# A second load of x and the cut of the last output-weight loads, in a one-core attention and expert decode kernel

Two small things were changed in a long kernel: the residual's x is taken from rows that are already on chip instead of being loaded a second time, and the last two blocks of the output weight are loaded in halves.

## Chip, cores and metric

One core of one Trainium2 chip. The metric is device time in microseconds (us), the median of several executions. Most executions of a kernel agree within 0.3%; the verdict "faster" or "slower" needs 2%.

## The reference, cut to what matters

Four tokens (B = 4), D = 1024, 32 heads of 128, a cache of 8192 positions per head, an expert with F = 3584. One token attends to the whole cache, so K and V are read once each: 537 MB of the 576 MB that the kernel reads.

```python
q = x @ wq                                    # (4, 32, 128)
p = softmax(q . k_cache * 128 ** -0.5)        # over 8192 positions
a = (p . v_cache) @ wo
y = (silu(x @ w_gate) * (x @ w_up)) @ w_down * sigmoid(x @ w_r)
b = x + y                                     # the residual
g = sigmoid((x * gate_w).sum(-1))
return g * a + (1 - g) * b
```

The change touches the term `(1 - g) * x` and the end of the product with `wo`.

## The kernel before

All large loads go through one ring of five 4 MB slots (`slot()`), and all of them are issued by SyncE's sequencer (`nc.sync.dma_start`), one after the other in the order of the built program. A K piece or a V piece covers two heads and fills one slot. VectorE transposes a K piece in four steps into buffers `T` of the pool `ttp`, which has two buffers under one tag; TensorE multiplies each transposed part into `S_ps`. After every eighth K piece a softmax follows.

```python
ring = ctx.enter_context(tc.tile_pool(name="ring", bufs=5))
ttp = ctx.enter_context(tc.tile_pool(name="ttp", bufs=2))
...
x6 = ttp.tile([NX, D], BF, name="x6", tag="T")
nc.scalar.dma_start(out=x6[0:Bn], in_=x2)              # x, used at the start
...
def k_piece(u):
    ...
    kn = slot()
    nc.sync.dma_start(out=kn[:], in_=kv_view(A_k_cache, u))
    for c in range(JR // CJ):                          # four steps
        T = ttp.tile([P, CJ, 2, 32, 2], BF, name="T", tag="T")
        nc.vector.transpose(out=T[:]..., in_=kn[:, c * CJ * Dh:(c + 1) * CJ * Dh]...)
        ...                                            # 8 matmuls into S_ps
    if t == GT - 1:
        softmax(g)
```

The residual is added once, in mid-kernel, after K piece 32, the first of a group of heads. It loads x again, into a buffer of the same two-deep pool:

```python
def add_x():
    xs = ttp.tile([Bn, 3 * D], BF, name="xs", tag="T")
    xb, xf = xs[:, 0:D], xs[:, D:3 * D].bitcast(F32)
    nc.sync.dma_start(out=xb, in_=x2)
    nc.vector.tensor_copy(out=xf, in_=xb)
    for n in range(NH):
        mm_acc(acc[:, n * NB:(n + 1) * NB], dg[:], xf[:, n * NB:(n + 1) * NB])
...
    if (kind, u) == ("k", NT // 2):
        add_x()
```

At the end, eight blocks of `wo` (1 MB each, four rows `r` per partition) are multiplied by the attention output. Each row takes two matmuls. The last block comes as three rows and one row:

```python
last = [wo_block(g) for g in range(2, NWB - 1)]
last += [wo_block(NWB - 1, 0, FR - 1), wo_block(NWB - 1, FR - 1, FR)]
...
for use in last:
    use()
```

## Time and profile before

| | before |
|---|---|
| median | 1360.24 us (1360.13 to 1360.25, three executions; a fourth, in the table of the result below, took 1360.83) |
| profiled execution | 1359.36 us, span 1357.7 us |
| read from HBM | 575.69 MB, 424 GB/s over the span |
| busy: TensorE, VectorE | 78%, 47% |

Two parts of the profile page of the kernel before. The first lines are the span and the busy time of the engines; the two rows below cut the span into 40 equal slices (33.9 us each), DMA being the busy share of the 16 DMA engines in tenths, GB/s what they moved.

```profile
span 1357.7 us, 8253 instructions
...
PE 1061.2 (78%) x4600; PEld 231.9 (17%) x2412; DVE 631.8 (47%) x375; ACT 41.5 (3%) x46; POOL 48.1 (4%) x115
...
DMA  9999999999999999997999999999999999999998
GB/s 406 427 431 430 431 431 432 431 430 432 430 430 432 431 432 431 433 430 342 385 432 433 431 427 431 431 429 430 432 432 432 432 431 431 432 430 430 431 426 338
```

The stream of loads is the bound: 430 to 433 GB/s in nearly every slice. Slices 19 and 20 (342 and 385) are a hole in the middle, slice 40 is the end.

The waits of the sequencer that issues the loads, in the kernel before: issue line, what it waited for, total us, times, longest.

```profile
engine line waited for: us in total, times, longest us
SPq L396 <- DVE T L338: 540.2, 55, 20.4
SPq L335 <- PE o_ps L403: 424.1, 50, 9.1
...
SPq L208 <- DVE T L338: 42.4, 1, 42.4
...
SPq L208 <- PE S_ps L344: 2.3, 1, 2.3
```

The first two rows look large and are harmless: a sequencer that waits for a ring slot while four other loads are under way loses nothing. The reload of x (L208) waited once, for 42.4 us and then 2.3 us more, with fewer loads under way than usual, as the timeline of the same sequencer shows (start, duration, what was issued). What it waited for is its buffer: the trace has the end of the third transpose of K32 at 644.88 us, and of the matmuls that read it at 647.24 us.

```profile
590.62 0.33 SPq L335 DMA_DIRECT2D piece<-in_A_k_cache_dram  x1
602.19 0.33 SPq L396 DMA_DIRECT2D piece<-in_A_v_cache_dram  x1
647.27 0.32 SPq L208 DMA_DIRECT2D xs<-in_A_x_dram  x1
647.64 0.35 SPq L335 DMA_DIRECT2D piece<-in_A_k_cache_dram  x1
648.05 0.42 SPq L396 DMA_DIRECT2D piece<-in_A_v_cache_dram  x1
648.51 0.43 SPq L335 DMA_DIRECT2D piece<-in_A_k_cache_dram  x1
649.04 0.46 SPq L396 DMA_DIRECT2D piece<-in_A_v_cache_dram  x1
```

K32 was issued at 590.62 and V24 at 602.19. Then the reload stood at the head of the order until 647.27. The four loads behind it left within 2 us of it, so their slots had been free for some time.

What that did to the stream, in stretches (length, busy time of each engine, granted clock, DMA share, GB/s), kernel before:

```profile
core 0: us, PE busy (x) PEld busy (x) DVE busy (x) ACT busy (x) POOL busy (x), PEclk, DMA share, GB/s
400.00:634.00 234.00, 190.68 (x792) 42.03 (x407) 115.83 (x67) 6.56 (x9) 6.36 (x17) 0.92 1.00 431
634.00:655.00 21.00, 15.37 (x60) 4.34 (x37) 10.03 (x7) 1.73 (x1) 2.52 (x3) 0.78 0.51 204
655.00:700.00 45.00, 35.34 (x145) 7.02 (x72) 18.02 (x8) 0.00 (x0) 0.53 (x2) 0.92 1.00 431
```

And the end, TensorE's matmuls with the last blocks of `wo` (start, duration, matmuls, in brackets the idle time before and what ended it):

```profile
1350.92 3.75 PE L188 MATMUL acc<-piece,LT 128*4 128x512 bf16 x16 [0.59 <-DMA piece<-in_A_wo_dram]
```

Block 6 and both parts of block 7 run as one row of 16 matmuls.

### The profile page before, as it was taken

The numbers are of one execution on the slowest core, as the hardware profiler recorded it, in microseconds if no ns is written. First come the engines' busy times: TensorE is split into PE (matmuls) and PEld (weight loads), VectorE is DVE, ScalarE is ACT, GpSimd is POOL, SyncE is SP. The second block draws the span as 40 slices with busy tenths as digits, with TensorE's granted clock in tenths as the row PEclk, the third lists the DMA queues.
The fourth block names the chain that finished last, engine by engine and source line by source line (L and its number), as shares of the span: only waits on it lengthen the run. The fifth ranks groups of instructions, "written<-read, shape, count | busy, mean of one in ns | idle before, by whom it ended". The sixth has DMA issues, their size and how long they took to land.

```text
span 1357.7 us, 8253 instructions
## 1 busy us (share of the span) xinstructions
PE 1061.2 (78%) x4600; PEld 231.9 (17%) x2412; DVE 631.8 (47%) x375; ACT 41.5 (3%) x46; POOL 48.1 (4%) x115
## 2 busy tenths in 40 slices
PE   3667779876988879886877769788787859887778
PEld 1111111211111111211111111111111112111111
DVE  3555654545544455445354455445454445456000
ACT  0000010001000000001000010000100010000000
POOL 2000000000000000000000000000000000000000
PEclk9878889887989979898988989898799988989999
DMA  9999999999999999997999999999999999999998
GB/s 406 427 431 430 431 431 432 431 430 432 430 430 432 431 432 431 433 430 342 385 432 433 431 427 431 431 429 430 432 432 432 432 431 431 432 430 430 431 426 338
DMA packets 22025, 576.23 MB, mean 424 GB/s; under 512 B 2386, under 2 KB 2394, under 8 KB 2660
## 3 DMA queue, kind: packets, MB, share of 16 engines
q1 hardware_dynamic: 21968, 575.69, 98.8%
q8 instruction: 27, 0.44, 0.1%
q14 instruction: 10, 0.08, 0.0%
q10 hardware_dynamic: 20, 0.02, 0.0%
HBM read 575.69 MB, written 0.01 MB: 424 GB/s over the span
## 4 chain that ended last, share of the span: by engine, by line
DMA 49%; PE 31%; DVE 12%; issue 6%; POOL 1%; ACT 1%; SPq 0%; DVEq 0%; ACTq 0%
DMA piece<-in_A_k_cache_dram 42%; PE o_ps L403 15%; PE S_ps L344 14%; DVE T L338 10%; DMA piece<-in_A_v_cache_dram 5%; DMA piece<-in_A_wo_dram 1%; PE small L421 1%; POOL PB L375 1%; DVE PT L369 1%; ACT PTs L367 1%; ACT OS L413 1%; DVE OS L414 1%; PE acc L188 0%; POOL tot L379 0%; DVE m L355 0%
## 5 line engine op out<-in xcount | busy, mean ns | idle before, releaser
L338 DVE STREAM_TRANSPOSE T<-piece 128x2048 uint32<-128x2048 uint32 x256 | 576.2, 2289 | 444.8 <-DMA piece<-in_A_k_cache_dram 292.6
L344 PE MATMUL S_ps<-T,Z 128*128 128x512 bf16 x2048 | 549.6, 419 | 252.4 <-DVE T L338 241.9
L403 PE MATMUL o_ps<-piece,PB 128*16 128x512 bf16 x2048 | 455.0, 380 | 17.2 <-DMA piece<-in_A_v_cache_dram 17.2
L344 PEld LDWEIGHTS <-Z 128*128 128x128 bf16 x1024 | 108.5, 106 | 677.7 <-issue 674.7
L403 PEld LDWEIGHTS <-PB 128*16 128x16 bf16 x1024 | 91.6, 90 | 373.7 <-issue 361.9
L414 DVE SCALAR_TENSOR_TENSOR OS<-o_ps,mE,OS 128x512 f32<-128x512 f32 x16 | 12.0, 751 | 175.8 <-ACT OS L413 175.8
L328 POOL TENSOR_TENSOR Z<-qa,mq 128x16 bf16<-128x16 bf16 x64 | 16.8, 264 | 1084.7 <-PE S_ps L344 1067.0
L413 ACT ACTIVATE OS<-o_ps,mE 128x512 f32<-128x512 f32 x16 | 11.0, 687 | 1049.0 <-PE o_ps L403 1049.0
L421 PEld LDWEIGHTS small<-selg,OS 128*128 128x128 f32 x128 | 22.9, 253 | 12.0 <-issue 11.1
L421 PE MATMUL small<-selg,OS 128*128 128x8 f32 x128 | 20.6, 288 | 0.0
L355 DVE TENSOR_REDUCE m<-S_ps 128x1 f32<-128x1024 f32 x8 | 9.8, 1225 | 15.9 <-PE S_ps L344 15.9
L188 PE MATMUL acc<-piece,LT 128*4 128x512 bf16 x64 | 14.9, 378 | 1.9 <-DMA piece<-in_A_wo_dram 1.8
L375 POOL COPY PB<-PT 64x1024 bf16<-64x1024 bf16 x8 | 15.1, 1889 | 28.8 <-DVE rex L377 28.8
L374 ACT COPY PB<-PT 64x1024 bf16<-64x1024 bf16 x8 | 15.3, 1909 | 10.6 <-DVE PT L369 10.6
L369 DVE STREAM_TRANSPOSE PT<-PTs 128x1024 bf16<-128x1024 bf16 x8 | 10.0, 1245 | 12.0 <-ACT PTs L367 12.0
L188 PE MATMUL acc<-piece,hT 128*4 128x512 bf16 x56 | 12.4, 379 | 0.0
L131 PE MATMUL small<-identb,x 6*128 6x6 bf16 x8 | 0.6, 192 | 14.1 <-DVE identb L128 14.1
L381 DVE RECIPROCAL rinv<-tot 128x16 f32<-128x16 f32 x8 | 2.0, 253 | 19.9 <-POOL tot L379 19.9
L367 ACT ACTIVATE PTs<-S_ps,negm 128x1024 bf16<-128x1024 f32 x8 | 8.9, 1114 | 70.8 <-DVE negm L364 70.8
L227 PE MATMUL S_ps<-piece,xw 128*4 128x512 bf16 x64 | 7.2, 626 | 2.7 <-DMA piece<-in_A_wq_dram 2.7
L424 DVE SCALAR_TENSOR_TENSOR OT<-small,sgb,rinv 128x8 bf16<-128x8 f32 x16 | 3.2, 202 | 10.2 <-PE small L421 10.2
L360 POOL PARTITION_ALL_REDUCE gmx<-mex x8 | 3.1, 392 | 79.7 <-issue 42.1
(72 smaller groups left out, 75.7 us busy)
## 6 DMA issues: line engine op xcount, KB each, us to landing
piece<-in_A_k_cache_dram SPq DMA_DIRECT2D x64, 4096.0 KB, 39.1
piece<-in_A_v_cache_dram SPq DMA_DIRECT2D x63, 4096.0 KB, 38.4
piece<-in_A_wq_dram SPq DMA_DIRECT2D x2, 4096.0 KB, 22.1
piece<-in_B_w_gate_dram SPq DMA_DIRECT2D x2, 3584.0 KB, 39.7
piece<-in_B_w_up_dram SPq DMA_DIRECT2D x2, 3584.0 KB, 33.9
piece<-in_A_wo_dram SPq DMA_DIRECT2D x7, 1024.0 KB, 27.3
piece<-in_B_w_down_dram SPq DMA_DIRECT2D x1, 4096.0 KB, 36.3
piece<-in_A_v_cache_dram SPq DMA_DIRECT2D x4, 1024.0 KB, 32.6
```

Of the source, the lines that this page charges most:

```text
L188: nc.tensor.matmul(out_ap, lhsT=lhsT, rhs=rhs, start=start, stop=True, skip_group_check=True)
L328: nc.gpsimd.tensor_tensor(out=Z[:, :, 31:31 + P].rearrange("p e (s d c) -> p e s d c", s=HT, d=QH)[:, :, :, :, 0], in0=qa[:, :, h0:h0 + HT ...
L338: nc.vector.transpose(out=T[:].rearrange("p j h i e -> p (j h i e)").bitcast(U32), in_=kn[:, c * CJ * Dh:(c + 1) * CJ * Dh].bitcast(U32))
L344: nc.tensor.matmul(sps[:, z, :], lhsT=Z[:, he, s:s + P], rhs=T[:, 16 * z:16 * z + 16, half, :, e], start=(t == 0 and c == 0 and he == 0), ...
L367: nc.scalar.activation(out=PTs[:], in_=sps[:].rearrange("p z n -> p (z n)"), func=ACT.Exp, bias=negm[:, 0:1], scale=scale, accum_out=rs[:, ...
L369: nc.vector.transpose(out=PT[:].rearrange("p j i -> p (j i)"), in_=PTs[:])
L374: nc.scalar.copy(out=Bv[0:W, :, :, 0, :], in_=Pv[0:W])
L375: nc.gpsimd.tensor_copy(out=Bv[W:P, :, :, 1, :], in_=Pv[W:P])
L403: nc.tensor.matmul(o_ps[row:row + NM, e, :], lhsT=B_[:, JT * t + c, z, w].rearrange("p e s j -> p (e s j)"), rhs=vn[:, j0 * Dh:(j0 + 4) * ...
L413: nc.scalar.activation(out=o_sb[:], in_=o_ps[:, 0, :], func=ACT.Copy, scale=mE[:, 0:1])
L414: nc.vector.scalar_tensor_tensor(out=o_sb[:], in0=o_ps[:, 1, :], scalar=mE[:, 1:2], in1=o_sb[:], op0=ALU.mult, op1=ALU.add)
L421: nc.tensor.matmul(oT[:, :], lhsT=o_sb[:, q * Dh:(q + 1) * Dh], rhs=selg[:, q].rearrange("p t s -> p (t s)"), start=(q == 0), stop=(q == 3))
```

## The change

The intent: no second load of x, so that nothing but ring loads stands in the load order; and less work after the last landing.

```diff
-    x6 = ttp.tile([NX, D], BF, name="x6", tag="T")
+    x6 = const.tile([NX, D], BF)
...
     def add_x():
-        xs = ttp.tile([Bn, 3 * D], BF, name="xs", tag="T")
-        xb, xf = xs[:, 0:D], xs[:, D:3 * D].bitcast(F32)
-        nc.sync.dma_start(out=xb, in_=x2)
-        nc.vector.tensor_copy(out=xf, in_=xb)
+        xf = ttp.tile([Bn, D], F32, name="xf", tag="T")
+        nc.vector.tensor_copy(out=xf[:], in_=x6[0:Bn])
...
-    last = [wo_block(g) for g in range(2, NWB - 1)]
-    last += [wo_block(NWB - 1, 0, FR - 1), wo_block(NWB - 1, FR - 1, FR)]
+    last = [wo_block(g) for g in range(2, NWB - 2)]
+    last += [wo_block(g, r, r + FR // 2) for g in (NWB - 2, NWB - 1) for r in (0, FR // 2)]
```

Only the one load is gone and one more `wo` load is there.

## The prediction

> **What bounds the kernel.** The load stream. The slices of the profile page show the 16 DMA engines at 90% or more nearly everywhere, moving 430 to 433 GB/s (576 MB in all), while TensorE is busy 78% of the span and VectorE 47%. The Trainium skill, "DMA: Bandwidth & Descriptors", section "Specifications", gives a fabric ceiling of 435 GB/s; the trace agrees to 1%. Time is won only where the stream pauses: at the start (406 GB/s in slice 1), at the end (338 in slice 40), and in one hole in the middle (342 and 385 in slices 19 and 20).
>
> **The hole.** All K, V and weight loads are issued in order from one sequencer. The residual's reload of x (8 KB) stands in that order, and its destination is a buffer of the two-deep ring that the K transposes use. The waits of the DMA-issuing sequencer show that this one issue waited 42.4 + 2.3 us for VectorE and TensorE to get through the following K piece. The timeline of that sequencer: a V load at 602.19 us, then nothing until the x load at 647.27; four 4 MB loads follow within 1.8 us, so several ring slots had been free already. The stream ran dry at 640.6 us. The stretch 634 to 655 us moved 204 GB/s instead of 431: (431 - 204)/431 x 21 us = 11.1 us lost. From 655 to 700 us it is 431 again, so nothing is made up later. The same page, section "Anatomy of one DMA", says that semaphore waits happen on the issuing sequencer before dispatch; the trace agrees.
>
> **What the change does there.** It removes the load, its issue (0.32 us) and, above all, its wait at the head of the in-order issues. The cast (0.68 us) and four small matmuls (1.9 us) remain at the same places in VectorE's and TensorE's order, and lie under the stream. Other group boundaries, with the same softmax but no x load, keep 430 to 432 GB/s, so I expect no pause in place of the hole. Gain: 11.1 us, all on the critical path.
>
> **The tail.** Before, blocks 6 and 7 of wo come as 1 MB, 768 KB and 256 KB. Block 6 lands at 1350.88 us; its 8 matmuls and the 8 of block 7 run back to back from 1350.92 to 1354.67 (0.215 us apart); the last landings are at 1352.74 and 1353.38. With halves, TensorE has done four matmuls earlier, and the last four wait for the last landing instead: 1353.4 + 4 x 0.215 + 0.2 = 1354.5. Gain 0.2 us; between -0.5 and +0.6. The additional issue costs nothing: loads are issued 15 us ahead.
>
> **Sum.** 1360.24 - 11.1 - 0.2 = 1348.9 us, 0.8% less. Range 1346.5 to 1352.0. Faster by over 2%: 1%; within 2%: 98%; slower by over 2%: 1%.
>
> **What would show it right.** Slices 19 and 20 at 430 or more; K and V issues near 611 and 629 us where none was; mean rate 427 GB/s; in the tail, the last four matmuls follow a DMA wait.
>
> **What would make it wrong.** A pause that remains at this softmax boundary, with cast and matmuls in it, would leave several us. Another chip whose steady rate differs by 0.3% moves the time by 4 us. In the tail, 4 KB rows might stream worse than 6 or 8 KB ones, below 1 us.

## The result, and the profile after

| | before | after |
|---|---|---|
| median | 1360.24 us (1360.13 to 1360.83) | 1349.57 us (1349.41 to 1349.65) |
| profiled execution | 1359.36 us, span 1357.7 us | 1349.57 us, span 1347.8 us |
| HBM rate over the span | 424 GB/s | 427 GB/s |

The medians differ by 10.67 us. The ratio is 0.9921 (95% interval 0.9903 to 0.9938); such ratios are the mean time of one kernel's fast runs over that of the other's in the same rounds, so not quite the ratio of the medians. The interval excludes 1.

The rows of slices of the page, after:

```profile
DMA  9999999999999999999999999999999999999997
GB/s 403 433 433 422 433 430 430 432 433 430 430 433 430 430 431 434 429 431 432 433 428 432 433 430 430 433 431 429 432 434 429 428 433 434 429 428 434 432 423 323
```

Slices 19 and 20 are now 431 and 432. The waits of the load sequencer, after:

```profile
SPq L394 <- DVE T L336: 551.3, 57, 21.0
SPq L333 <- PE o_ps L401: 442.1, 52, 10.4
```

The long wait of L208 is gone, and the two waits for ring slots have grown by 11 and 18 us in total. Its timeline, after:

```profile
590.53 0.33 SPq L333 DMA_DIRECT2D piece<-in_A_k_cache_dram  x1
603.21 0.33 SPq L394 DMA_DIRECT2D piece<-in_A_v_cache_dram  x1
612.17 0.33 SPq L333 DMA_DIRECT2D piece<-in_A_k_cache_dram  x1
620.43 0.33 SPq L394 DMA_DIRECT2D piece<-in_A_v_cache_dram  x1
629.39 0.33 SPq L333 DMA_DIRECT2D piece<-in_A_k_cache_dram  x1
649.78 0.33 SPq L394 DMA_DIRECT2D piece<-in_A_v_cache_dram  x1
```

K33, V25 and K34 are now issued at 612, 620 and 629 us, where nothing was. The following gap of 20 us before V26 does no harm, because three pieces (K33, V25 and K34) are still under way when it ends. The stretch of the hole, after:

```profile
634.00:655.00 21.00, 15.74 (x52) 4.48 (x33) 13.17 (x9) 1.67 (x1) 2.45 (x3) 0.67 1.00 430
```

And the end, after:

```profile
1338.79 3.61 PE L188 MATMUL acc<-piece,LT 128*4 128x512 bf16 x16 [0.58 <-DMA piece<-in_A_wo_dram]
1342.57 1.02 PE L188 MATMUL acc<-piece,LT 128*4 128x512 bf16 x4 [0.17 <-DMA piece<-in_A_wo_dram]
1343.81 1.02 PE L188 MATMUL acc<-piece,LT 128*4 128x512 bf16 x4 [0.22 <-DMA piece<-in_A_wo_dram]
```

The two halves of block 7 are now waited for, 0.17 and 0.22 us each.

**Where 9.8 us went, execution against execution.** In the traces each large load raises its semaphore (the counter that those who need the data wait for) in 16 steps, which I take for one from each of the 16 DMA engines; the packed trace has the time of each step. From these come the first and the last landing of a load. No view of the profile prints them; the table is worked out from the traces of the two profiled executions.

| | before | after |
|---|---|---|
| V24, last of 16 engines landed | 640.6 us | 640.5 us |
| K33, last landed | 659.9 | 650.2 |
| last load of all, last landed | 1353.38 | 1343.77 |
| from there to the end of the span | 4.27 | 4.07 |

In a steady stream a piece lands 9.7 us after the one before. Before, K33 landed 19.36 us after V24, so the hole cost 9.65 us; at the last load the two kernels are 9.61 us apart. With 0.2 us at the end this makes 9.8 us; the two profiled executions differ by 9.79 us. The medians differ by 0.88 us more because the profiled execution of the kernel before was that much faster than its median.

### The profile page after: what moved, and what is told of

It reads as the page before. It is cut to its first block, busy times and chain, and to the rows that moved or that the text cites. A ratio compares the mean times of both kernels' runs of the same rounds, so it can differ in the third digit from the quotient of the medians.

```text
span 1347.8 us, 8253 instructions
## 1 busy us (share of the span) xinstructions
PE 1059.3 (79%) x4600; PEld 233.2 (17%) x2412; DVE 631.4 (47%) x375; ACT 41.5 (3%) x46; POOL 47.9 (4%) x115
## 4 chain that ended last, share of the span: by engine, by line
DMA 50%; PE 30%; DVE 11%; issue 6%; ACT 1%; POOL 1%; SPq 0%; DVEq 0%; ACTq 0%
DMA piece<-in_A_k_cache_dram 40%; PE o_ps L401 16%; PE S_ps L342 13%; DVE T L336 10%; DMA piece<-in_A_v_cache_dram 9%; PE small L419 1%; DMA piece<-in_A_wo_dram 1%; POOL PB L373 1%; DVE PT L367 1%; ACT PTs L365 1%; ACT OS L411 1%; DVE OS L412 1%; POOL tot L377 0%; PE acc L188 0%; PE o_ps L225 0%
## 5 line engine op out<-in xcount | busy, mean ns | idle before, releaser
L342 PEld LDWEIGHTS <-Z 128*128 128x128 bf16 x1024 | 108.0, 105 | 667.2 <-issue 664.3
L419 PEld LDWEIGHTS small<-selg,OS 128*128 128x128 f32 x128 | 24.9, 273 | 12.2 <-issue 11.1
L422 DVE SCALAR_TENSOR_TENSOR OT<-small,sgb,rinv 128x8 bf16<-128x8 f32 x16 | 3.2, 202 | 11.7 <-PE small L419 11.7
```

What stands on the lines that cost most here:

```text
L342: nc.tensor.matmul(sps[:, z, :], lhsT=Z[:, he, s:s + P], rhs=T[:, 16 * z:16 * z + 16, half, :, e], start=(t == 0 and c == 0 and he == 0), ...
L419: nc.tensor.matmul(oT[:, :], lhsT=o_sb[:, q * Dh:(q + 1) * Dh], rhs=selg[:, q].rearrange("p t s -> p (t s)"), start=(q == 0), stop=(q == 3))
```

## The experiments

Twelve runs were made, of nine different kernels, in three sets of four, each set on one chip beside the kernel before. All results were correct. In the order of the sets, the kernel before had medians of 1361.16 us (1358.78 to 1362.74), 1362.23 (1360.15 to 1364.05) and 1361.54 (1360.14 to 1362.73).

| run | kernel | median us | range |
|---|---|---|---|
| e1_control | the change | 1349.59 | 1349.34 to 1349.70 |
| e2_x_only | first part alone | 1349.49 | 1349.36 to 1349.80 |
| e3_tail_only | second part alone | 1360.19 | 1358.85 to 1360.69 |
| e4_tail_211 | the change, last block 2+1+1 rows | 1349.26 | 1349.18 to 1349.78 |
| e5_own_buffer | reload without a wait | 1349.47 | 1349.37 to 1349.78 |
| e6_act_queue | reload issued by ScalarE | 1349.48 | 1349.41 to 1349.50 |
| e7_mid_group | reload four K pieces later | 1355.23 | 1354.22 to 1356.36 |
| e8_before_again | before, one execution | 1363.81 | one run, state unknown |
| t1_whole | the change, last two blocks whole | 1350.03 | 1349.98 to 1350.27 |
| t2_three_one | the kernel of e2 again | 1349.55 | 1349.48 to 1349.65 |
| t3_halves | the change again | 1349.61 | 1349.46 to 1349.92 |
| t4_two_one_one | the kernel of e4 again | 1349.19 | 1348.95 to 1349.29 |

**The theory:** the reload waited for a buffer at the head of an in-order line of loads, and the stream behind it ran dry. **Rivals:** the reload itself (traffic, latency) disturbs the stream; VectorE and TensorE waiting for x make the hole; the pool's rotation, with x of the start in it, makes it; the gain comes from the tail.

### Which part of the change

e1 is the change as it stands. e2 has only the diff's parts for x, e3 only the last four lines of the diff.

> The changed kernel once more, as the control of this set. Theory (in-order issue): ratio to before 0.992, that is 10.5 to 11 us less, with both parts of the change in it. Rival (the chip or run differed): a ratio nearer to 1.

> Only the first part: x from the rows on chip, wo blocks 6 and 7 as before (1 MB, 768 KB, 256 KB). Theory: the whole gain is here, within 0.3 us of the control: 1349.6 us, 10.3 to 11.1 us below before; the 634 to 655 us stretch at 430 GB/s. The prediction's tail term says this is 0.2 us slower than the control; the profile of the changed kernel, in which the last 1 MB of the stream arrived 1.1 us late against the rest, allows the contrary: up to 0.9 us faster than the control.

> Only the second part: the reload of x stays, wo blocks 6 and 7 come in halves. Theory: 1360.0 us, -0.2 us from before (between -0.6 and +0.6), and the hole of 11 us near 640 us stays. If the gain came from the tail, 1349.6 us.

Measured: ratios to before of 0.9915, 0.9915 (0.9901 to 0.9928) and 0.9991 (0.9979 to 1.0004). The whole gain is in x. Set against the median of before on the same chip, e1 and e2 gained 11.6 and 11.7 us, more than the 10.5 to 11 and the 10.3 to 11.1 us that I had expected, since before scatters (below). e3 keeps the hole (208 GB/s from 634 to 655 us in its trace, and a wait of 42.4 + 2.1 us at the reload). The second part is worth nothing that these runs can tell.

### Load, wait or place

e5 starts from the change and puts the reload back on the same sequencer, into a buffer that nothing else uses:

```diff
+        xb = const.tile([Bn, D], BF, name="xb")
         xf = ttp.tile([Bn, D], F32, name="xf", tag="T")
-        nc.vector.tensor_copy(out=xf[:], in_=x6[0:Bn])
+        nc.sync.dma_start(out=xb[:], in_=x2)
+        nc.vector.tensor_copy(out=xf[:], in_=xb[:])
```

> The second load of x is back, on the same sequencer and at the same place in its order, but into a buffer of its own, so that it waits for no engine. Theory (the wait at the head of the in-order issues made the hole): no hole, 1349.6 us, within 0.3 us of the changed kernel. Rival (the load itself, its 8 KB in small packets and its latency, disturbs the stream): 1360 us.

Measured: 1349.47 us; the reload was issued at 591.0 us, and the stretch 634 to 655 us ran at 429 GB/s:

```profile
634.00:655.00 21.00, 15.58 (x62) 4.34 (x38) 14.26 (x9) 1.53 (x1) 2.31 (x3) 0.79 1.00 429
```

The load itself costs nothing, although it landed only at 630.3 us, 39.3 us after its issue and within a microsecond of the K piece issued just before it. One thing more differs from the kernel before: here the built program has the reload ahead of V24, as the source has it; before, it stood behind V24. A reload without a wait at exactly the old place was not run; e6 leaves the order of the large loads as it was.

e6 starts from the kernel before (with `wo` in halves) and changes one word:

```diff
-        nc.sync.dma_start(out=xb, in_=x2)
+        nc.scalar.dma_start(out=xb, in_=x2)
```

> The second load of x is as before, into the two-deep ring and with x of the start in that ring too, but ScalarE's sequencer issues it. Its wait is then the same, some 40 us, but nothing of the stream stands behind it. Theory: no hole, 1349.6 us, within 0.5 us of the changed kernel, although VectorE still waits 1 to 3 us for the landing. Rivals (VectorE's and TensorE's wait for x, or the ring's rotation with x in it, made the hole): 1360 us.

Measured: 1349.48 us, 428 GB/s from 634 to 655 us:

```profile
634.00:655.00 21.00, 12.28 (x40) 3.77 (x24) 9.60 (x8) 1.91 (x1) 2.59 (x3) 0.67 1.00 428
```

The instructions on the tile of x in this run (line, engine, duration in ns min/median/max, first and last start; below, VectorE's idle time that ended with the landing):

```profile
L208 ACTq DMA_DIRECT2D xs<-in_A_x_dram x1: 254/254/254, 649.7 to 649.7; - x1
L209 DVE CAST xs<-xs x1: 682/682/682, 655.9 to 655.9; 4x1024 f32<-4x1024 bf16 x1
...
  DMA xs<-in_A_x_dram: 5.7, 1
```

Issued at 649.7, x was not cast until 655.9: the landing took about 6 us beside the running stream, VectorE waited 5.7 us for it and TensorE's weight load 5.2 us for VectorE. In the kernel before these two waits were 1.1 and 0.6 us, and I had expected 1 to 3 us here; the longer ones cost nothing in the total. So the compute engines' wait and the pool's rotation are not the cause: here x of the start is in the pool as before. Only the place of the wait, in front of the stream's loads, is left.

e7 also starts from the kernel before with halves, and moves the addition:

```diff
-        if (kind, u) == ("k", NT // 2):
+        if (kind, u) == ("k", NT // 2 + 4):
```

> The second load of x is as before (ring, same sequencer), but the addition of x stands four K pieces later, in the middle of a group of heads, where no softmax holds VectorE up between the landing of the K piece and its transposes. wo in halves. Theory: the sequencer still waits until the K piece is nearly computed, some 9.5 us after it landed, when the next V piece has just landed (9.7 us later), so a short hole stays: about 2.2 us in the last landings, 1351.8 us (1350.5 to 1354). Rival (any second load costs the same 10 us wherever it stands): 1360 us. The spread between the first and the last of the 16 engines to land a load should fall to about 0.5 us after this hole, and be 3 to 3.5 us at the end.

Measured: 1355.23 us. The rival "10 us wherever it stands" is wrong, but so was my number; the runs, from 1354.22 us on, touch neither 1351.8 nor the range up to 1354 that I gave. The load sequencer and the stretches around the reload:

```profile
681.68 0.33 SPq L396 DMA_DIRECT2D piece<-in_A_v_cache_dram  x1
721.78 0.33 SPq L208 DMA_DIRECT2D xs<-in_A_x_dram  x1
722.16 0.34 SPq L335 DMA_DIRECT2D piece<-in_A_k_cache_dram  x1
```

```profile
700.00:710.00 10.00, 7.36 (x34) 1.53 (x17) 1.83 (x2) 0.69 (x1) 0.26 (x1) 0.99 0.99 426
710.00:724.00 14.00, 12.27 (x40) 3.71 (x23) 8.69 (x6) 0.00 (x0) 0.00 (x0) 0.64 0.55 216
```

V28 landed last at 718.5 us, and the reload left at 721.78, 12.9 us after VectorE had begun to transpose K36 (708.92); I had expected 9.5 us from the landing. TensorE's granted clock was 0.64 in that stretch, where I had counted on full clock. The next piece landed at 734.35, 6.1 us later than a steady stream would have brought it. The sign and the order of the mechanism hold; the size depends on a compute speed that I took from a favourable stretch.

### Why the kernel before scatters and the changed one does not

> The kernel before once more, for a second trace of it: in the set with the control its runs lay between 1358.8 and 1362.7 us, while those of the changed kernel lay within 0.4 us. Theory: the hole's length varies with the compute it waits for, so its last-landing loss is 9.7 us plus whatever this run is above 1359.4 us, within 0.4 us; the stream elsewhere is the same within 0.3 us.

Measured: 1363.81 us, 4.45 us above the profiled execution of before. Its reload left at 651.90 us, 4.63 us later than before's 647.27. V24 landed last at 640.5 and K33 at 664.3: with the steady 9.7 us taken off, the hole cost 14.1 us, against 9.7 + 4.45 = 14.15 expected. Without their holes the two spans are the same, 1348.0 us, so the stream elsewhere did not differ, as expected. TensorE around the K piece that the reload waits for, in the profiled execution of before and then in e8:

```profile
638.96 3.57 PE L344 MATMUL S_ps<-T,Z 128*128 128x512 bf16 x8 [9.55 <-DVE T L338]
642.33 1.43 PE L421 MATMUL small<-selg,OS 128*128 128x8 f32 x8
643.61 3.63 PE L344 MATMUL S_ps<-T,Z 128*128 128x512 bf16 x16
```

```profile
641.20 3.57 PE L344 MATMUL S_ps<-T,Z 128*128 128x512 bf16 x8 [9.54 <-DVE T L338]
644.57 1.71 PE L421 MATMUL small<-selg,OS 128*128 128x8 f32 x8
646.13 5.73 PE L344 MATMUL S_ps<-T,Z 128*128 128x512 bf16 x16
```

The piece started 2.2 us later in e8, and stayed at half clock longer. The clock records of the trace (the share of the full TensorE clock that was granted, with the time of each change) give a stretch at 0.5 from 633.08 to 643.32 us in the first and from 636.79 to 650.44 us in the second. The late start goes back to the clock too: in e8 a stretch at 0.5 from 612.90 to 619.72 us lies on the matmuls of K31, which ended 2.2 us later than in before, where the clock was full (means of 0.69 and 1.00 from 611 to 622 us). The Trainium skill, "TensorE: Matmul & The Clock Gate", section "Part 1: The HAM clock gate", says that an idle window of about 3.4 us brings the half rate, that a busy one ends it, and that the window runs free of the kernel. These traces agree: the stretches at 0.5 are 10.24 and 13.65 us long, three and four times 3.41, after TensorE had been idle for some 9.5 us during the softmax. One busy window did not always end it: in e8 the clock rose 9.2 us after the first matmul, though TensorE was busy without a break from 642 to 650 us; in before it rose 4.4 us after it. In the kernel before, the length of the hole is set by this compute, so in these two traces the clock accounts for the 4.6 us between the two reloads, and so for the difference of the totals. The trace of e3, which has the hole too, fits: 10.24 us at half clock, the reload at 647.03, 1358.85 us in all. That the whole scatter of before, from 1358.78 to 1364.05 us in the three sets, comes from there is likely but not shown: its other executions were not traced, and no run held the clock. The changed kernel and e2, e5 and e6, in which nothing in the load order waits that way, all lie between 1349.3 and 1349.9. e8 is a single execution; its sums are taken inside one trace.

### The skew of the 16 engines

From the same landings: time between the first and the last of the 16 engines to land one load.

| us between first and last landing | near 630 to 640 us | next load | near 1290 us |
|---|---|---|---|
| before (hole at 640) | 3.4 | 0.5 | 3.5 |
| after | 3.4 | 3.4 | 6.6 |
| e7 (hole at 718) | 3.4 | 3.7 | 3.3 |

A hole brings the engines together; I read it so that the fast ones run out of work first and wait. In e7 the spread fell from 3.6 to 0.6 us at its hole, and grew to 3.3 again, as expected. The growth is not steady. In before the spread stands at 2.0 us from 700 to 1089 us and at 3.5 us from 1110 us on; between, one load adds 1.6 us, and after the hole one load (landed at 700.26) adds 1.5 us. Each of these two steps meets a packet of 16 KB on another queue, at 1098.1 and 694.6 us. The page counts such packets as instruction loads (queue and kind, packets, MB, share of the engines):

```profile
q8 instruction: 27, 0.44, 0.1%
q14 instruction: 10, 0.08, 0.0%
```

In the traces of before, after and all twelve runs, each of the 109 steps of more than 0.15 us (from 60 us on) has one of these packets, of 8 or 16 KB, between the first landing of the load before and the last landing of its own. Of all 1998 loads in these traces only 667, a third, have one there. So instruction loads go with the drift; that they cause it is not shown, as no run changed them. The spread is why the mean rate overstates the hole: in the stretch 634 to 655 us the bytes missing are worth 11.1 us, but part of it is fast engines stopping up to 3.4 us early, and those were ahead anyway. What counts is the last engine, 9.6 us. By bytes, the changed kernel is 10.9 us ahead at 574 MB and only 9.6 us ahead at the last landing of a load; the 1.3 us is the larger spread at its end (6.5 against 3.5 us).

### The tail, all cuts on one chip

The edits to the changed kernel, for t1 and t4 (e4):

```diff
-    last = [wo_block(g) for g in range(2, NWB - 2)]
-    last += [wo_block(g, r, r + FR // 2) for g in (NWB - 2, NWB - 1) for r in (0, FR // 2)]
+    last = [wo_block(g) for g in range(2, NWB)]                            # t1
+    last = [wo_block(g) for g in range(2, NWB - 2)]                        # t4
+    cuts = [(NWB - 2, 0, 2), (NWB - 2, 2, 4), (NWB - 1, 0, 2), (NWB - 1, 2, 3), (NWB - 1, 3, 4)]
+    last += [wo_block(*cut) for cut in cuts]
```

> The changed kernel with the last wo block cut in 2, 1 and 1 rows instead of 2 and 2: after the last landing two matmuls remain instead of four (0.215 us each), so 0.4 us less than the control if the last landing is what the end waits for and does not move: 1349.2 us. If more and smaller loads at the end land later, no gain or a loss of some tenths.

> The changed kernel with wo blocks 6 and 7 each loaded whole (1 MB). Theory of the tail: eight matmuls, 0.215 us apart, follow the last landing instead of four, so 0.86 us more than the changed kernel: 1350.4 us. If the end is not bound by the last landing plus its matmuls: 1349.5 us.

> x from the rows on chip, last block 3 rows and 1 row as in the kernel before (the same kernel as the run with the first part alone), again beside the others. Theory: the eight matmuls of block 7 run behind those of block 6 and end 1.28 us after the last landing began to be usable, against 1.07 us with halves: 0.2 us more than the changed kernel; the earlier set showed no difference (1349.49 against 1349.59 us).

> The changed kernel again, as the control of this set: 1349.5 us.

> Last block in 2, 1 and 1 rows, again beside the others. Theory: two matmuls after the last landing instead of four, 0.3 to 0.4 us less than the control of this set; the earlier set showed 0.33 us.

| last block | last landing us | to the start of the last matmul | to the end of the span | median us |
|---|---|---|---|---|
| whole (t1) | 1343.54 | 1.55 | 4.74 | 1350.03 |
| 3 + 1 (t2) | 1343.71 | 0.91 | 4.21 | 1349.55 |
| halves (t3) | 1343.81 | 0.69 | 4.06 | 1349.61 |
| 2 + 1 + 1 (t4) | 1343.90 | 0.26 | 3.68 | 1349.19 |

The number of matmuls after the last landing does what was expected: halves against whole is 0.86 us up to the last matmul, of which 0.68 us is left at the end of the span. But each finer cut of these four had its last landing 0.1 to 0.2 us later in its trace. The other traces of the same kernels do not settle whether that is chance: 1343.76 for 3 + 1 (e2), 1343.57 and 1343.77 for halves (e1 and the changed kernel), 1343.90 for 2 + 1 + 1 (e4). In the medians, whole costs 0.42 us, not 0.86; 3 + 1 and halves cannot be told apart (0.06 and, in the first set, 0.10 us in favour of 3 + 1, inside ranges of 0.2 to 0.5 us). The cut 2 + 1 + 1 is 0.42 us below halves, with ranges that do not meet; in the first set it was 0.33 us, with one of its four runs above the control's. It is the version that beats both kernels, the changed one by a few tenths.

## Why the prediction was right, point by point

- **The bound and the cause: right.** The time went where the stream paused; the cuts at the end are worth tenths. e5 and e6 take away the wait at the head of the loads and nothing else of weight, and each gives the whole gain. The prediction rests here on the Trainium skill, "DMA: Bandwidth & Descriptors", "Anatomy of one DMA" (a wait for a semaphore happens on the issuing sequencer). That section is written for DMAs issued by GpSimd; here it is SyncE that issues, and the waits of L208 (42.4 + 2.3 us) and its timeline agree.
- **The size of the hole: the term "11.1 us lost" was mis-sized.** It was taken from the mean rate. The last engine lost 9.6 us in that execution. Of this error of 1.5 us, 0.9 us was covered, by luck, by another: I took the hole of an execution of 1359.36 us off a median of 1360.24 us, whose hole should by e8 be longer. 1359.36 - 9.6 - 0.2 = 1349.56 us is the sum that should have been written; 1349.57 us was measured.
- **No pause in place of the hole: right.** 430 GB/s from 634 to 655 us.
- **The signs to look for: right.** Slices 19 and 20 at 431 and 432, issues at 612 and 629 us, a mean of 427 GB/s, and the last four matmuls behind a DMA wait.
- **The tail, "0.2 us": not confirmed.** In the profiled pair the end came 0.20 us sooner after the last landing, as computed (in t2 and t3 0.15 us); in the medians, two sets show no gain from halves over 3 + 1.
- **Not foreseen:** that the kernel before scatters over 5 us and the changed one over half a microsecond, and that a hole resets the engines' skew.

Open: whether the instruction loads are what drives the 16 engines apart, and whether the bytes could be shared out so that they end together. No run tried that. Nor was the hole of an execution at exactly the median traced.

## What to carry to other kernels

In a kernel bound by its loads, look at the order in which the loads are issued, not only at their bytes: one small load that waits for a compute buffer holds up all loads behind it, and the cost is that wait minus the time that the loads already under way still last. Put such a load on another sequencer, give it a buffer of its own, or do without it. Measure a pause of the stream by the last landings before and after it, and take sums from one execution, not half from a profile and half from a median.

## What the Trainium skill lacked or had wrong

- "DMA: Bandwidth & Descriptors", "Issuing engines are not separate DMA queues": it says that issuing from several engines only saves the time it takes to initiate a DMA. In e6 another sequencer took over a load whose issue lasts 0.32 us, and what it saved was the wait before that issue, which held up the loads behind: 1349.48 us against 1362.23 us for the kernel before on the same chip (the cut of `wo`, which e6 has too, is worth nothing in e3).
- The same page, no section has a figure for it: a load of 8 KB issued from a second sequencer beside a running stream took about 6 us until it could be used (e6, 649.7 to 655.9 us); the same load into a dry stream took 1.7 us (before, 647.27 to 648.93 us), and behind other loads on their own sequencer 39.3 us (e5, 591.0 to 630.3 us).
- The same page, no section: the 16 engines drift apart under a steady stream of equal loads, from 3.4 us near 640 us to 6.6 us near 1290 us (the changed kernel), by steps of up to 1.6 us that come with instruction loads on other queues, and a pause brings them back to 0.5 us (before).
- "TensorE: Matmul & The Clock Gate": it has the free-running window, but not the case in which loads wait for TensorE, so that the clock can lengthen a pause of the stream: 1359.36 us with 10.24 us at half clock there (before), 1363.81 us with 13.65 us (e8), and 1349.3 to 1349.9 us for the kernels in which no load waits that way.
